# Final feed-forward of a two-layer decode kernel: statistics by small matmuls, column halves in two PSUM banks, a new order of the work

## The chip, the cores and the metric

The kernel runs on one core of one Trainium2 chip. The metric is the device time of one execution in microseconds, as the median of several runs. Engines are named as in the profile: PE is the matrix engine TensorE (PEld its weight loads), DVE is VectorE, ACT is ScalarE, POOL is GpSimd, and SP is SyncE, whose queue issues all the loads here.

## What is computed

Two layers of a decode step for a batch of 8 rows of width 448. Each layer is attention with a cached window, and then a feed-forward with SiLU. Both layers use the same weights and the same cache.

```python
x = A_x                                             # (8, 1, 448), bf16
x = x + _A_ref(_layernorm(x), k_cache, v_cache, wq, wo)
x = x + _B_ref(_layernorm(x), w1, w2)
x = x + _A_ref(_layernorm(x), k_cache, v_cache, wq, wo)
x = x + _B_ref(_layernorm(x), w1, w2)               # the final feed-forward

# _layernorm: (x - mean) / sqrt(var + 1e-5), no scale or shift
# _A_ref: 16 query heads, 8 key/value heads of 256, the last 1024 of 4096 positions;
#         softmax(q k^T / 16) v, then wo (4096 x 448)
# _B_ref: silu(x @ w1) @ w2 with w1 (448 x 1792) and w2 (1792 x 448)
```

Keys and values of the window are 8 rows x 8 heads x 1024 x 256 in bf16, each, which is 64 loads of 512 KB for the keys and 64 for the values. Each is read from HBM once and used by both layers.

## The kernel before

**Rows and layers.** For each batch row b the program builds `layer1(b)` and then `layer2(b)` (L953 to L957). `layer1` transposes the row's key tiles on DVE (L914), computes scores (L641), softmax (`softmax`, L652), the value products (`pv_rows`, L685, and `pv_cols`, L719), and the output projection (`wo_part`, L762). `layer2` begins with `chain` (L793), which holds the first feed-forward of that row and the queries of layer 2, then come scores, softmax and value products of layer 2. All of this is for one row, so matmuls have one or two active columns in the stationary operand and are packed four to the array by `tile_position`. The second output projection and the final feed-forward are done at the end for all eight rows together, in `final_wo` (L835) and `final_rows` (L846).

**The load queue.** Key and value loads go in a fixed sequence into 30 slots of SBUF. A load waits until the tile that was in its slot has been used by both layers. Weights are loaded once, at the beginning.

**What sets the order.** Nothing is ordered by hand. Each step is a `Task` with an engine, a modelled duration, and keys that it reads and writes. PSUM is tracked by whole banks: a step that reads a bank waits for other engines' earlier readers of that bank too (L69 to L75). `Plan.schedule` (L91) is a list scheduler. It gives each task a rank, the length of the modelled path behind it, adds a constant per kind of task (`BIAS`, L25), and lets an engine hold back for a more urgent task that will be ready within `HOLD` times the duration of the one at hand (L24, L141). The resulting order of each engine is emitted as it stands, with semaphore waits between engines. So a change in the tasks, in `OCC` (modelled durations), `BIAS`, `HOLD` or the `rate` of a load can move instructions anywhere in the kernel. Loads keep their sequence.

**Filler matmuls.** `keep` (L773) and `idle` (L779) issue matmuls of zeros that keep TensorE active while it would wait. `keep` writes bank SC[1] and `idle` a bank that it is given.

**The end, step by step.** Eight banks of 512 fp32 columns: SC = 0 and 1 (scores of layers 1 and 2), OB = 2 and 3 (value products), LB = 4 and 5, XB = 6, YB = 7. STB is bank 5.
- `final_wo` sets up the residual in YB (L837) and projects the attention output of all rows, 449 columns in XB, in two parts of 16 matmuls, for the first and the second half of the heads (L839). Column 449 holds the negative mean of the row.
- ACT copies XB to SBUF (L847). Six matmuls fold the four partial sums and turn them into columns (`to_cols`, L537). DVE copies the mean (L852), adds it (L854) and masks (L857), which gives the centred rows `xbt8`.
- `stats8` (L547) computes the variance: squares on ACT (L549), a split in two bf16 parts on DVE (L550, L551), eight matmuls with ones (L556), a scaling (L568), and `pow` on POOL for 128x8 elements (L570), `rhalf8`.
- `up` (L514) multiplies by w1 (16 packed matmuls of 448 columns, L516), ACT copies (L524), five matmuls turn the rows into columns (L527, L529).
- DVE multiplies by `rhalf8` (L861), ACT takes tanh (L864), DVE forms the SiLU (L865).
- 14 packed matmuls multiply by w2 (L867), five bring the residual to XB (L873, L876), ACT copies the product (L878), one matmul adds it to the residual (L879), DVE copies the sum to SBUF (L881), and SP writes it out (L882).

The row sums of w2 and wo, which make the extra column of means, are computed once near the beginning (`row_sums`, L439).

Of the kernel before, what the change touches and what calls it, by code (L numbers as in the profile page):

```python
# [19 lines left out]
       "pe:idle": 0.2296, "act:maskr": 0.13, "act:qbd1": 0.19, "act:var4": 0.16, "act:x2b": 0.16, "act:yrow": 0.50, "act:rsum": 0.66,  # L20
# [3 lines left out]
HOLD, PE_SCALE = 0.563, 1.062  # L24
BIAS = {"dve.KT.a": -19.0, "pe.S0.1.a": 41.7, "pe.oT.a": 213.9, "pe.stat.b": 285.2, "pe.qturn.b": 293.1,  # L25
        "pe.qsel.b": 221.3, "pe.S1.0.b": 186.2, "dve.mb.c": 47.4, "act.exp.c": 84.8, "dve.rl.c": 176.4,
        "pe.PV1.0.1.c": 178.2, "pe.oT.c": 209.3, "pe.idle.e": -29.9}
# [220 lines left out]
def bass_interleave_layers__sliding_block_cached__dense_activation_silu__decode_kernel(  # L248
# [9 lines left out]
    P = 128  # L258
# [64 lines left out]
    z8 = t0f.bitcast(F32)[:, 0:FC * NB]  # L323
    th8 = t1f.bitcast(F32)[:, 0:FC * NB]
    hT8 = t1f[:, 256:256 + FC * NB]
    xbt8 = t1f[:, 400:400 + XC * NB].rearrange("p (c b) -> p c b", b=NB)
# [77 lines left out]
    def load_wq():  # L404
        for c in range(3):
            dma(lambda e, c=c: e.dma_start(wq_sb[:, c * HD:(c + 1) * HD], A_wq[c * P:(c + 1) * P, :]),
                [("wq", c)], P * HD * 2, "wq%d" % c, rate=410e3)
        for h in range(2):
            dma(lambda e, h=h: e.dma_start(wq_sb[64 * h:64 * h + 64, 3 * HD:], A_wq[3 * P:D, h * HD2:(h + 1) * HD2]),
                [("wq", 3 + h)], 32 * HD * 2, "wq%d" % (3 + h), rate=250e3)  # L410

    def load_w1():
        dma(lambda e: e.dma_start(w1_sb[:, 0:3 * F].rearrange("p (c n) -> p c n", c=3),
                                  B_w1[0:3 * P, :].rearrange("(c p) n -> p c n", p=P)),
            [("w1", 0)], 3 * P * F * 2, "w1", rate=390e3)
        for h in range(2):
            dma(lambda e, h=h: e.dma_start(w1_sb[64 * h:64 * h + 64, 3 * F:], B_w1[3 * P:D, h * F2:(h + 1) * F2]),
                [("w1", 1 + h)], 32 * F * 2, "w1%d" % h, rate=250e3)

    def load_wo():  # L420
        dma(lambda e: e.dma_start(wo_sb[:].rearrange("p (c n) -> p c n", n=DP)[:, :, 0:D],
                                  A_wo.rearrange("(c p) n -> p c n", p=P)), ["wo"], HD * D * 2, "wo", rate=380e3)

    def load_w2():
        rows = w2_sb[:].rearrange("p (c n) -> p c n", n=DP)[:, :, 0:D]
        parts = B_w2.rearrange("(j r) n -> j r n", j=4)
        for j in range(4):
            dma(lambda e, j=j: e.dma_start(rows[:, 3 * j:3 * j + 3, :],  # L428
                                           parts[j, 0:3 * P, :].rearrange("(c p) n -> p c n", p=P)),
                [("w2", j)], 3 * P * D * 2, "w2%d" % j, rate=400e3)  # L430
        for h in range(2):
            dma(lambda e, h=h: e.dma_start(rows[64 * h:64 * h + 64, 12:14, :],
                                           parts[h:4:2, 3 * P:D, :].rearrange("j p n -> p j n")),
                [("w2", 4 + h)], P * D * 2, "w2%d" % (4 + h), rate=250e3)
# [4 lines left out]
    def row_sums(w, key, groups, prio):  # L439

        needs = ([("w2", j) for j in range(6)] if key == "w2" else [key]) + H8
# [72 lines left out]
    def up(x, nb, bi, col, reads, prio, fresh):  # L514

        pe([lambda e, c=c, j=j: e.matmul(  # L516
            bank[XB][32 * j:32 * j + nb, 0:D], x(xcol(c, j // 2)), w1_r(j, c), start=(c == 0), stop=(c == KC - 1),
            tile_position=(0, 32 * j), skip_group_check=True) for c in range(KC) for j in range(4)],
           reads + W1_R, bk(XB) + ["part"], (D, 4), prio, "w1")
        if nb == 1:  # L520
            keep(2, prio, "part")
        else:
            idle(2, prio, "part", SC[0])
        act(lambda e: e.activation(qrow[:, 0:D], bank[XB][:, 0:D], ACTF.Copy), bk(XB), ["rowb"], 0.6, prio, "yrow")  # L524
        y = bank[bi][:, col:col + FC * nb].rearrange("p (f b) -> p f b", b=nb)
        pick = ident[:].rearrange("p (j b) -> p j b", b=32)[:, :, 0:nb]
        fns = [lambda e, c=c: e.matmul(y[:, c:12:3, :], qrow[:, c * P:(c + 1) * P], pick, start=fresh, stop=True,  # L527
                                       skip_group_check=True) for c in range(3)]
        fns += [lambda e, h=h: e.matmul(y[64 * h:64 * h + 64, 12:14, :], qrow[:, 3 * P:D], pick[:, h:4:2, :], start=fresh,  # L529
                                        stop=True, tile_position=(0, 64 * h), skip_group_check=True) for h in range(2)]  # L530
        pe(fns, ["rowb", "ident"], bk(bi) + ["turned"], (4 * nb, 1), prio, "yturn")
        if nb == 1:
            keep(2, prio, "turned")
        else:
            idle(4, prio, "turned", SC[0])

    def to_cols(bank_i, col, row, rhs, nb, prio, reads, name, shape):  # L537
        fns = [lambda e, c=c: e.matmul(bank[bank_i][xpart(c), col + c * nb:col + (c + 1) * nb], xpiece(row, c), rhs,  # L538
                                       start=False, stop=True, tile_position=xpos(c), skip_group_check=True)
               for c in range(XC)]  # L540
        fns.append(lambda e: e.matmul(bank[bank_i][:, col + XC * nb:col + (XC + 1) * nb],
                                      row[:, D:D1].broadcast_to([P, P]), rhs, start=False, stop=True,
                                      skip_group_check=True))
        pe(fns, reads, bk(bank_i) + ["folded"], shape, prio, name)


    def stats8(xp, reads, prio, mean):  # L547
# [7 lines left out]
               for c in range(KC)] if mean else []  # L555
# [4 lines left out]
        if mean:  # L560
            dve(lambda e: e.tensor_scalar(nmean8, s1, -1.0 / D, None, op0=ALU.mult), bk(STB), [("qbd", 0, 1)], 0.17, prio)
            dve(lambda e: e.tensor_tensor(vn8, s1, nmean8, ALU.mult), bk(STB) + [("qbd", 0, 1)], [("qbd", 0, 1)], 0.17,
                prio)
            dve(lambda e: e.tensor_tensor(vn8, s2, vn8, ALU.add), bk(STB) + [("qbd", 0, 1)], [("qbd", 0, 1)], 0.17, prio)
            dve(lambda e: e.tensor_scalar(vn8, vn8, D * EPS, 4.0 / D, op0=ALU.add, op1=ALU.mult), [("qbd", 0, 1)],
                [("qbd", 0, 1)], 0.12, prio)
        else:
            dve(lambda e: e.tensor_scalar(vn8, s2, D * EPS, 4.0 / D, op0=ALU.add, op1=ALU.mult), bk(STB),  # L568
                [("qbd", 0, 1)], 0.17, prio)
# [3 lines left out]
    def start_rows(prio):  # L573
# [7 lines left out]
        stats8(xb0[:, 0:XC, :], ["xb0"], prio, True)  # L581
# [103 lines left out]
    def pv_rows(b, layer, k2, prio, oT_dst, oT_key, nj=4):  # L685

        ob, lb, ei = OB[layer], LB[layer], layer
# [105 lines left out]
    def chain(b, prio):  # L793
        xcols(prio)
        stats(YB, C_S2, prio)
        up(lambda c: xbt[:, c:c + 1], 1, YB, C_W1, ["xbt"], prio, False)
# [38 lines left out]
    def final_wo(k2, prio):  # L835
        if k2 == 0:
            pe(lambda e: e.matmul(x8, ident[:], x2b[:].rearrange("p c b -> p (c b)"), start=True, stop=True),  # L837
               ["ident"] + [("x2b", b) for b in range(NB)], bk(YB), (100, 1), prio, "xinit8")
        pe([lambda e, i=i: e.matmul(  # L839
            bank[XB][32 * (i % 4):32 * (i % 4) + NB, 0:D1], oT2[:, i % 2, i // 2, :], wo_sb[:, i * DP:i * DP + D1],  # L840
            start=(i < 4), stop=(i >= NCH - 4), tile_position=(0, 32 * (i % 4)), skip_group_check=True)
            for i in range(16 * k2, 16 * k2 + 16)],
           [(("oT2", b), 2 * h) for b in range(NB) for h in range(4 * k2, 4 * k2 + 4)] + WO_R, bk(XB) + ["part"], (D, 4),
           prio, "wo8")

    def final_rows(prio):  # L846
        act(lambda e: e.activation(rowb, bank[XB][:, 0:D1], ACTF.Copy), bk(XB), ["rowb"], 0.54, prio, "rowb8")  # L847
        idle(2, prio, "part", SC[0])
        to_cols(YB, C_X8, rowb, fold8[:], NB, prio, ["rowb", ] + FOLD8, "fold8", (120, 1))
        idle(2, prio, "folded", SC[0])  # L850
        m58 = mask5[:].unsqueeze(2).broadcast_to([P, XC, NB])
        dve(lambda e: e.tensor_copy(nm8[:], x8[:, XC * NB:]), bk(YB), ["nm8"] + H8, 0.17, prio)  # L852
        xcf = big8[:, 0:XC * NB].rearrange("p (c b) -> p c b", b=NB)
        dve(lambda e: e.tensor_tensor(xcf, x8[:, 0:XC * NB].rearrange("p (c b) -> p c b", b=NB),  # L854
                                      nm8[:].unsqueeze(1).broadcast_to([P, XC, NB]), ALU.add), bk(YB) + ["nm8"], B8, 0.22,
            prio)
        dve(lambda e: e.tensor_tensor(xbt8[:], xcf, m58, ALU.mult), B8 + M5, ["xbt8"], 0.2, prio)  # L857
        stats8(xbt8[:], ["xbt8"], prio, False)
        up(lambda c: xbt8[:, c, :], NB, OB[1], 0, ["xbt8"], prio, True)
        z = z8.rearrange("p (f b) -> p f b", b=NB)  # L860
# [128 lines left out]
```

## Time and profile before

| | us |
|---|---|
| median of 7 runs | 263.03 |
| lowest and highest of them | 261.37, 263.39 |
| the profiled execution's own time | 263.78 |
| its span (first to last instruction) | 262.0 |

| engine | busy us | share of the span | instructions |
|---|---|---|---|
| PE | 197.2 | 75% | 3746 |
| PEld | 101.2 | 39% | 3746 |
| DVE | 153.5 | 59% | 410 |
| ACT | 87.8 | 34% | 241 |
| POOL | 12.8 | 5% | 25 |

The profile is one execution. Its span is shorter than its own time by the 1.78 us before the first and after the last instruction. The loads move 77.67 MB from HBM and are busy in nearly all of the first 222 us; the last 40 us have only compute. PE's busy time includes the filler matmuls (L775 and L782, 33.6 us). A group of instructions is named by its line, its engine and its tiles; "idle before" is the time that the engine stood still ahead of them, with what ended it. The chain is the work that ended last, followed back from the last instruction, at each step to what released it.

### The profile page before, as it was taken

The numbers are of one execution on the slowest core, as the hardware profiler recorded it, in microseconds if no ns is written. First come the engines' busy times: TensorE is split into PE (matmuls) and PEld (weight loads), VectorE is DVE, ScalarE is ACT, GpSimd is POOL, SyncE is SP. The second block draws the span as 40 slices with busy tenths as digits, with TensorE's granted clock in tenths as the row PEclk, the third lists the DMA queues.
The fourth block names the chain that finished last, engine by engine and source line by source line (L and its number), as shares of the span: only waits on it lengthen the run. The fifth ranks groups of instructions, "written<-read, shape, count | busy, mean of one in ns | idle before, by whom it ended". The sixth has DMA issues, their size and how long they took to land.

```text
span 262.0 us, 8450 instructions
## 1 busy us (share of the span) xinstructions
PE 197.2 (75%) x3746; PEld 101.2 (39%) x3746; DVE 153.5 (59%) x410; ACT 87.8 (34%) x241; POOL 12.8 (5%) x25
## 2 busy tenths in 40 slices
PE   0053212399878987999899799979988997998784
PEld 0051100143444454444444454544445444533431
DVE  6468657806964874786388468738863974202221
ACT  2002346624232523441443325244323433132221
POOL 1200000000000000000000000000000000000001
PEclk9999999999999999999999999999999999799999
DMA  6999999999999999998999899999999997000000
GB/s 239 350 403 375 311 339 349 361 362 407 356 354 407 378 317 345 409 361 273 381 402 350 269 405 379 303 319 408 361 293 375 402 350 237 3 3 3 0 3 1
DMA packets 50227, 78.21 MB, mean 299 GB/s; under 512 B 2304, under 2 KB 41104, under 8 KB 49808
## 3 DMA queue, kind: packets, MB, share of 16 engines
q1 hardware_dynamic: 50192, 77.68, 85.1%
q8 instruction: 29, 0.48, 0.8%
q14 instruction: 6, 0.05, 0.0%
HBM read 77.67 MB, written 0.01 MB: 296 GB/s over the span
## 4 chain that ended last, share of the span: by engine, by line
PE 62%; DVE 9%; ACT 9%; SPq 8%; DMA 7%; issue 3%; POOL 1%; DVEq 0%; ACTq 0%
PE bank L699 13%; PE bank L641 13%; DMA wo_sb<-in_A_wo_dram 7%; PE bank L775 6%; PE bank L816 6%; SPq L428 5%; PE bank L768 5%; ACT qbd L662 4%; PE bank L516 3%; DVE qbd L447 3%; PE bank L803 2%; ACT qrow L823 2%; DVE mseg L648 2%; PE bank L709 2%; PE bank L538 2%
## 5 line engine op out<-in xcount | busy, mean ns | idle before, releaser
L914 DVE STREAM_TRANSPOSE slot<-slot 128x512 uint32<-128x512 uint32 x128 | 82.1, 686 | 5.4 <-DMA slot<-in_A_k_cache_dram 5.0
L699 PE MATMUL bank<-slot,pT_sb 128*2 128x256 bf16 x960 | 41.3, 286 | 9.3 <-DMA slot<-in_A_v_cache_dram 8.5
L641 PE MATMUL bank<-slot,qbd 128*8 128x256 bf16 x1024 | 39.7, 284 | 7.0 <-DVE slot L914 6.1
L699 PEld LDWEIGHTS bank<-slot,pT_sb 128*2 128x2 bf16 x960 | 19.7, 84 | 21.5 <-DMA slot<-in_A_v_cache_dram 10.2
L641 PEld LDWEIGHTS bank<-slot,qbd 128*8 128x8 bf16 x1024 | 21.3, 85 | 15.3 <-DVE slot L914 7.2
L662 ACT ACTIVATE qbd<-bank,mseg 128x256 bf16<-128x256 f32 x32 | 12.7, 472 | 37.6 <-DVE mT L654 27.9
L707 ACT ACTIVATE qbd<-bank 128x256 bf16<-128x256 f32 x32 | 12.2, 382 | 30.8 <-PE bank L699 29.3
L648 DVE TENSOR_REDUCE mseg<-bank 128x1 f32<-128x256 f32 x32 | 13.5, 424 | 14.1 <-PE bank L641 13.4
L768 PE MATMUL bank<-wo_sb,oT 128*1 128x449 bf16 x256 | 19.9, 379 | 1.9 <-DVE wo_sb L450 1.9
L775 PE MATMUL bank<-wq_sb,cols_b 128*128 128x512 bf16 x64 | 20.5, 404 | 0.0
L753 POOL TENSOR_TENSOR rhalf<-var,nhalf 128x1 f32<-128x1 f32 x16 | 8.7, 542 | 219.9 <-ACT var L751 219.9
L667 PE MATMUL bank<-ident,qbd 128*128 128x128 bf16 x64 | 6.6, 227 | 16.3 <-ACT qbd L662 16.3
L610 ACT ACTIVATE qbd<-bank,mask 128x128 bf16<-128x128 f32 x32 | 12.2, 381 | 18.3 <-PE bank L605 17.5
L680 DVE TENSOR_REDUCE l_sb<-bank 128x16 f32<-128x64 f32 x16 | 3.6, 225 | 23.4 <-PE bank L675 23.4
L816 PE MATMUL bank<-wq_sb,xbt 128*1 128x512 bf16 x256 | 16.7, 378 | 0.6 <-DVE xbt L742 0.6
L713 DVE TENSOR_TENSOR oT<-bank,l_sb 128x16 bf16<-128x16 f32 (+1 forms) x32 | 6.5, 202 | 16.3 <-PE bank L709 16.0
L782 PE MATMUL bank<-wq_sb,cols_b 128*128 128x512 bf16 x49 | 13.1, 381 | 0.0
L823 ACT ACTIVATE qrow<-bank 128x512 bf16<-128x512 f32 x16 | 9.6, 597 | 9.2 <-PE bank L816 9.2
L667 PEld LDWEIGHTS bank<-ident,qbd 128*128 128x128 bf16 x64 | 3.7, 99 | 22.0 <-ACT qbd L662 22.0
L447 DVE TENSOR_REDUCE qbd<-wo_sb 128x5 f32<-128x2240 bf16 x4 | 9.7, 2479 | 3.7 <-DMA wo_sb<-in_A_wo_dram 3.7
L788 ACT ACTIVATE qrow<-bank 128x449 bf16<-128x449 f32 x8 | 4.4, 548 | 18.1 <-PE bank L768 18.1
L624 DVE TENSOR_TENSOR qbd<-bank,maskr 128x256 bf16<-128x256 f32 x16 | 6.8, 425 | 5.5 <-PE bank L619 5.1
(135 smaller groups left out, 214.8 us busy)
## 6 DMA issues: line engine op xcount, KB each, us to landing
slot<-in_A_k_cache_dram SPq DMA_DIRECT2D x64, 512.0 KB, 10.4
slot<-in_A_v_cache_dram SPq DMA_DIRECT2D x64, 512.0 KB, 8.7
wo_sb<-in_A_wo_dram SPq DMA_DIRECT2D x1, 3584.0 KB, 17.6
wq_sb<-in_A_wq_dram SPq DMA_DIRECT2D x3, 1024.0 KB, 6.9
w_sb<-in_B_w_dram SPq DMA_DIRECT2D x4, 336.0 KB, 15.9
w_sb<-in_B_w_dram SPq DMA_DIRECT2D x1, 1344.0 KB, 11.3
wq_sb<-in_A_wq_dram SPq DMA_DIRECT2D x2, 256.0 KB, 10.2
w_sb<-in_B_w_dram SPq DMA_DIRECT2D x4, 112.0 KB, 8.7
```

The costliest lines, as they stand in the source:

```text
L428: dma(lambda e, j=j: e.dma_start(rows[:, 3 * j:3 * j + 3, :], parts[j, 0:3 * P, :].rearrange("(c p) n -> p c n", p=P)), [("w2", j)], 3 * P ...
L447: dve(lambda e, view=view, n=n, row=row: e.tensor_reduce(row[:, 0:n], view[:, :, 0:D], AX.X, ALU.add, negate=True), needs, [("sums", key, ...
L641: fns.append(lambda e, cb=cb, par=par, j=j, kvh=kvh, kv=kv: e.matmul(bank[sc][32 * j:32 * j + 8, k2 * 256:(k2 + 1) * 256], qbd[qi][:, kvh, ...
L648: dve(lambda e: e.tensor_reduce(mseg[layer][:, k2:k2 + 1], bank[sc][:, k2 * 256:(k2 + 1) * 256], AX.X, ALU.max, negate=True), bk(sc), [("m ...
L662: act(lambda e, k2=k2: e.activation(e_sb[ei][:, k2, :, :].rearrange("p uh (jj ul) -> p uh jj ul", ul=4), bank[sc][:, k2 * 256:(k2 + 1) * 2 ...
L699: fns.append(lambda e, q=q, uh=uh, j=j, vv=vv: e.matmul(bank[ob][32 * j:32 * j + 2, c0:c0 + DH], pT_sb[ei][:, k2 * 2 + uh, j * 8 + 2 * q:j ...
L768: fns.append(lambda e, i=i, c=c, kvh=kvh: e.matmul(bank[XB][32 * c:32 * c + 1, 0:D1], oT1[:, i % 2, i // 2:i // 2 + 1], wo_sb[:, i * DP:i ...
L775: pe([lambda e: e.matmul(bank[SC[1]][:], zero_b.broadcast_to([P, P]), wq_sb[:, 0:512], start=False, stop=True, skip_group_check=True) for ...
L782: pe(lambda e: e.matmul(bank[bi][:], zero_b.broadcast_to([P, P]), wq_sb[:, 0:512], start=False, stop=True, skip_group_check=True), [("wq", ...
L816: pe([lambda e, j=j, c=c, k2=k2, wb=wb: e.matmul(bank[wb][32 * j:32 * j + 1, :], xbt[:, xcol(c, k2):xcol(c, k2) + 1], wq_sb[:, c * HD + (( ...
L823: act(lambda e, wb=wb: e.activation(qrow[:], bank[wb][:], ACTF.Copy), bk(wb), ["rowb"], 0.55, prio, "qrow")
L914: dve(lambda e, v=v: e.transpose(v, v), [("slot", s)], [("slot", s)], 0.67, prio, "KT")
```

## The change

In `final_wo` and `final_rows`:
- The output projection, the product with w1 and the product with w2 are each computed in two column halves, 0 to 255 in one bank and the rest in another (XB or OB[0], and SC[1]). ACT copies the first half and DVE the second (`two`).
- The mean is added by TensorE: one more matmul in `to_cols`, which broadcasts the mean column over all column groups, and one more in the setup of the residual. DVE then only masks.
- The variance comes from 16 small matmuls of the centred rows with themselves (`gram8`); DVE picks the diagonal with an accumulating instruction (`diag8`); POOL takes the power of one column instead of eight.
- The deviation is applied as the scale of the copies of the w1 product (`yrow8`), per row, before the rows are turned into columns. tanh and SiLU then read PSUM.
- The residual and the last sum are in two halves too, in XB and YB, and both engines copy them.

Outside of the final part: the second value half of layer 2 of the last row uses bank OB[0] instead of OB[1]; the row sums also wait for `q1T`; `OCC`, `HOLD`, `BIAS` and the modelled rates of the weight loads have new values.

```diff
@@ planner constants
-HOLD, PE_SCALE = 0.563, 1.062
-BIAS = {"dve.KT.a": -19.0, "pe.S0.1.a": 41.7, "pe.oT.a": 213.9, "pe.stat.b": 285.2, "pe.qturn.b": 293.1,
-        "pe.qsel.b": 221.3, "pe.S1.0.b": 186.2, "dve.mb.c": 47.4, "act.exp.c": 84.8, "dve.rl.c": 176.4,
-        "pe.PV1.0.1.c": 178.2, "pe.oT.c": 209.3, "pe.idle.e": -29.9}
+HOLD, PE_SCALE = 0.837, 1.062
+BIAS = {"dve..e": -51.1, "pe.qsel1.a": -37.9, "pe.S0.0.a": -128.5, "act.exp.a": -58.6, "pe.l.a": 18.8, "act..a":
+        -106.8, "act.oev.a": -58.1, "pe.oT.a": 43.2, "pe.wo.a": -42.9, "pe.stat.b": 263.8, "pe.qturn.b": 188.6,
+        "pe.qsel.b": 262.3, "dve.max.b": 218.8, "dve.mT.c": 118.3, "dve.mg.c": 108.3, "dve.mb.c": 87.2,
+        "act.pTev.c": -93.6, "act.oev.c": -59.6, "pe.oT.c": -79.9, "pe.PV1.1.0.c": -83.7, "pe.PV1.1.2.c":
+        -139.0, "pe.PV1.1.3.c": -36.7, "pe.wo8.c": -95.5, "pe.idle.e": -7.4, "dve.nm8.e": -11.1, "pe.xres.e":
+        -10.8}
@@ load_w1, for one (wq, wo and w2 likewise)
-            [("w1", 0)], 3 * P * F * 2, "w1", rate=390e3)
+            [("w1", 0)], 3 * P * F * 2, "w1", rate=340e3)
@@ row_sums
-        needs = ([("w2", j) for j in range(6)] if key == "w2" else [key]) + H8
+        needs = ([("w2", j) for j in range(6)] if key == "w2" else [key]) + H8 + ["q1T"]
@@ to_cols
+        if nb > 1:
+            fns.append(lambda e: e.matmul(
+                bank[bank_i][:, col:col + XC * nb].rearrange("p (c b) -> p c b", b=nb), row[:, D:D1].broadcast_to([P, P]),
+                rhs.unsqueeze(1).broadcast_to([P, XC, nb]), start=False, stop=True, skip_group_check=True))
@@ pv_rows
-        ob, lb, ei = OB[layer], LB[layer], layer
+        ob, lb, ei = OB[layer] if b < NB - 1 or k2 == 0 else OB[0], LB[layer], layer
@@ final_wo
+        for half, bi, n0, n1 in ((0, XB, 0, 256), (1, SC[1], 256, D1)):
+            pe([lambda e, i=i, bi=bi, n0=n0, n1=n1: e.matmul(
+                bank[bi][32 * (i % 4):32 * (i % 4) + NB, n0:n1], oT2[:, i % 2, i // 2, :],
+                wo_sb[:, i * DP + n0:i * DP + n1], start=(i < 4), stop=(i >= NCH - 4), tile_position=(0, 32 * (i % 4)),
+                skip_group_check=True) for i in range(16 * k2, 16 * k2 + 16)],
...
+    def two(ba, bb, n, dst, keys, prio, name, scale=None):
+
+        sc = 1.0 if scale is None else scale[:, 0:1]
+        rd = [] if scale is None else ["rhalf"]
+        act(lambda e: e.activation(dst[:, 0:256], bank[ba][:, 0:256][0:dst.shape[0]], ACTF.Copy, scale=sc), bk(ba) + rd,
+            [keys[0]], 0.42, prio, name)
+        dve(lambda e: e.tensor_scalar(dst[:, 256:n], bank[bb][:, 256:n][0:dst.shape[0]], sc, None, op0=ALU.mult),
+            bk(bb) + rd, [keys[1]], 0.36, prio, name)
@@ final_rows
-        act(lambda e: e.activation(rowb, bank[XB][:, 0:D1], ACTF.Copy), bk(XB), ["rowb"], 0.54, prio, "rowb8")
+        dve(lambda e: e.memset(g8, 0.0), [], bk(STB), 0.12, prio, "pick8")
+        dve(lambda e: e.memset(pick8, 4.0 / D), [], ["pick8"] + Z8, 0.12, prio, "pick8")
+        for q in range(4):
+            dve(lambda e, q=q: e.tensor_scalar(pick8[32 * q:32 * q + NB, :], fold8[32 * q:32 * q + NB, :], 4.0 / D, None,
+                                               op0=ALU.mult), FOLD8 + ["pick8"], [("pick8", q)], 0.12, prio, "pick8")
+        two(XB, SC[1], D1, qrow, ROW2, prio, "rowb8")
...
-        stats8(xbt8[:], ["xbt8"], prio, False)
-        up(lambda c: xbt8[:, c, :], NB, OB[1], 0, ["xbt8"], prio, True)
+        dve(lambda e: e.tensor_tensor(xbt8[:], x8[:, 0:XC * NB].rearrange("p (c b) -> p c b", b=NB), m58, ALU.mult),
+            bk(YB) + M5, ["xbt8"] + H8, 0.22, prio, "xbt8")
+        dve(lambda e: e.tensor_copy(nm8[:], x8[:, XC * NB:]), bk(YB), ["nm8"], 0.17, prio - 0.1, "nm8")
+        pe([lambda e, c=c, j=j: e.matmul(g8[32 * j:32 * j + NB, :], xbt8[:, c, :], xbt8[:, c, :], start=(c == 0),
+                                         stop=(c == KC - 1), tile_position=(0, 32 * j), skip_group_check=True)
+            for c in range(KC) for j in range(4)], ["xbt8"], bk(STB), (64, 1), prio, "gram8")
+        dve(lambda e: e.scalar_tensor_tensor(out=scr8, in0=g8, scalar=D * EPS, in1=pick8, op0=ALU.add, op1=ALU.mult,
+                                             accum_out=var4[:]), bk(STB) + [("pick8", q) for q in range(4)], ["var4"] + Z8, 0.2, prio, "diag8")
+        add("pool", lambda e: e.tensor_tensor(rhalf[:], var4[:], nhalf[:, 0:1], ALU.pow),
+            reads=["var4", "nhalf"], writes=["rhalf"], dur=0.4, prio=prio, name="pow")
+        for bi, n0, n1 in ((XB, 0, 256), (SC[1], 256, D)):
+            pe([lambda e, c=c, j=j, bi=bi, n0=n0, n1=n1: e.matmul(
+                bank[bi][32 * j:32 * j + NB, n0:n1], xbt8[:, xcol(c, j // 2), :], w1_r(j, c)[:, n0:n1], start=(c == 0),
+                stop=(c == KC - 1), tile_position=(0, 32 * j), skip_group_check=True) for c in range(KC) for j in range(4)],
+               ["xbt8"] + W1_R, bk(bi) + ["part"], (256, 4), prio, "w18")
...
+        two(XB, SC[1], D, qrow, ROW2, prio, "yrow8", rhalf)
+        turn(OB[1], 0, NB, ROW2, prio)
...
-        z = z8.rearrange("p (f b) -> p f b", b=NB)
-        dve(lambda e: e.tensor_tensor(z, bank[OB[1]][:, 0:FC * NB].rearrange("p (f b) -> p f b", b=NB),
-                                      rhalf8.unsqueeze(1).broadcast_to([P, FC, NB]), ALU.mult),
-            bk(OB[1]) + [("qbd", 0, 1)], Z8, 0.25, prio + 0.2)
+        act(lambda e: e.activation(th8, y, ACTF.Tanh), bk(OB[1]), D8, 0.3, prio + 0.2, "th8")
+        dve(lambda e: e.scalar_tensor_tensor(out=hT8, in0=th8, scalar=1.0, in1=y, op0=ALU.add, op1=ALU.mult),
+            bk(OB[1]) + D8, H8, 0.25, prio + 0.2, "hT8")
...
-        dve(lambda e: e.tensor_copy(orow, ops), bk(XB), B8, 0.5, prio + 0.3)
+        two(XB, YB, D, orow, H8, prio + 0.3, "out9")
```

## The prediction

> **What bounds the kernel now.** I read the page, then the chain of work that ended last, then the waits of the load queue, then the DMA rate over one batch row, then the clock in short stretches.
>
> The page gives the chain's shares:
>
> ```profile
> PE 62%; DVE 9%; ACT 9%; SPq 8%; DMA 7%; issue 3%; POOL 1%; DVEq 0%; ACTq 0%
> ```
>
> TensorE carries the chain, but with small matmuls and with hops to ScalarE and VectorE. Is it compute or the loads that set the pace of a row? The waits of the load queue and the DMA rate in 176 to 202 us (40 slices of 0.65 us, busy tenths and GB/s) answer:
>
> ```profile
> SPq L472 <- PE bank L641: 32.0, 7, 5.8
> ```
>
> ```profile
> DMA  9999999999999999999999999983499899989999
> GB/s 403 422 391 416 410 397 416 384 422 403 416 411 397 380 359 356 353 350 350 343 350 348 350 348 348 336 285 131 139 367 347 232 315 377 364 347 391 441 384 397
> ```
>
> The reader is to see the dip near 193.5 us. Once per row the loads run dry for over a microsecond, because the next V load waits until the layer-2 scores (L641) have released a K slot. So a row of about 23.9 us (the softmax exponentials start at 148.14, 172.01, 195.94 and 219.90) is a loop of compute, slot release and load, without slack. Work moved within this loop counts seven times, once for each period between rows.
>
> The last loads land near 222 us; after that only compute is left. Its end, in the chain in order of time (start, us, what):
>
> ```profile
> 247.62 0.39 ACT qbd L707
> ...
> 248.34 0.97 PE bank L699 x32
> ...
> 250.53 0.96 PE bank L839 x16
> 251.52 0.56 ACT qrow L847
> ...
> 252.63 0.18 DVE qbd L852
> 252.83 0.21 DVE qbd L854
> 253.07 0.21 DVE qbd L857
> ...
> 253.32 0.93 PE bank L516 x16
> 254.25 0.30 PE bank L556 x8
> 254.58 0.18 DVE qbd L568
> ...
> 254.82 1.66 POOL qbd L570
> ...
> 256.57 0.29 DVE qbd L861
> 256.88 0.30 ACT qbd L864
> ...
> 257.29 0.29 DVE qbd L865
> ...
> 257.62 0.94 PE bank L867 x14
> 258.58 0.55 ACT qrow L878
> ...
> 259.18 0.37 PE bank L879
> 259.57 0.61 DVE qbd L881
> ```
>
> One instruction at a time, no engine shared: what is cut here comes off the end in full. The power on GpSimd (L570, 1.66) is the longest piece; the first product has been turned into columns by 255.27, and its scaling (L861) waits for the power until 256.57.
>
> The clock, by stretches (us of the stretch; busy PE, PEld, DVE, ACT, POOL; granted clock; DMA share; GB/s):
>
> ```profile
> 223.00:223.50 0.50, 0.50 (x20) 0.35 (x12) 0.17 (x1) 0.00 (x0) 0.00 (x0) 0.50 0.00 0
> ```
>
> Half clock, from about 222.95 to 226.4. The last row goes from its first value products (221.85) to its first keep-warm pair (229.55) in 7.70 us; row 6 took 6.36 for the same (197.88 to 204.24). So this profile holds 1.34 us of slow clock.
>
> **What the Trainium skill says.** "PSUM — Partial Sum Buffer", on bank collisions: two engines may not touch one bank and 32-partition quadrant at once. So ScalarE and VectorE can share an evacuation only if the halves lie in two banks, as the change puts them; before, one engine reads 449 columns alone (L847, 0.55), and no trace here shows the shared case. "TensorEngine Tiling (Array Packing)", Key Properties: changing the tiling mode drains the array; the trace has idle gaps of 0.2 to 0.4 us put down to issue wherever packed and full-size matmuls alternate (before L709, L729, L775), so I add none between the new Gram matmuls and the packed w1, which share a mode. "TensorE: Matmul & The Clock Gate", Part 1: the clock is halved after a 3.4 us activity window that was too idle, and the windows run free of the kernel; the stretch above, 3.4 us long, agrees.
>
> **The change part by part.** First the unit prices. Sixteen packed matmuls of 256 columns took 0.61, thirty-two took 1.05: 27 ns each beyond the first group. Sixteen of 448 took 0.93. VectorE from PSUM: 0.42 for 256 columns (L648), 0.61 for 448 (L881), 0.17 for 16, so 0.16 + 1.0 ns a column, 0.36 for 192. ScalarE: 0.38 for 256 columns (L707), 0.55 for 449. A scale read from memory costs 0.09 more (L788: 0.55 without, 0.64 with; the skill's page "ScalarE: Activation LUTs", What ACT_TABLE_LOAD costs, says about 93 ns a pointer). The eight-column power took 1.64, the one-column power 0.54 (L753).
>
> *a) Last product of the output projection, its evacuation and centring (250.53 to 253.27, 2.74 us).* The product goes from 0.93 to about 1.05 (32 matmuls for 16). The ScalarE half starts at 0.61 and is covered by the second half; VectorE follows with 0.36 + 0.04 hop, ending at 1.45 against 1.54 now: -0.09. The row fold gets one matmul more, about +0.06 (six there are issued in about 0.35). Of three VectorE steps (L852, L854, L857, 252.63 to 253.27, 0.64) one is left, 40 columns from PSUM, 0.20: -0.44. The copy of the mean goes behind it, under the Gram matmuls. Together -0.47. The two filler matmuls behind the fold end their streaming about when the new operand is ready; if not, +0.1.
>
> *b) From the centred rows to the activated hidden rows (253.27 to 257.57, 4.30 us).* Gone: square, two VectorE steps, eight ones-matmuls, the 1.64 power, the scaling L861. New: 16 Gram matmuls (hop 0.05, then 0.60 as for sixteen small packed ones); the diagonal with its accumulator on VectorE. No row shows that operation. Below it is bounded by 0.17 (any eight-column VectorE row); above by 0.45 (the skill's "VectorE: DVE Perf Modes", Two Vector instructions with no wait between them, makes it two instructions; ScalarE's accumulator read took 0.19). I take 0.25, with 0.04 to start it. Then 0.07 + 0.54 for the one-column power and 0.05 hop: the deviation stands at 1.60. Meanwhile the two w1 halves follow the Gram matmuls and end near 1.53, so both are due together. Evacuation with the scale 0.47, hop 0.06, turn 0.37 (254.90 to 255.27), hop 0.04, tanh 0.30, hop 0.11, product 0.28: 3.23. Saving 1.07.
>
> *c) Second product to the output (257.62 to 260.18).* 28 matmuls for 14: +0.03. Evacuation 0.36 for 0.54: -0.18. Fold of 192 columns for 448: 0.25 for 0.35, -0.10. Last copy in two halves, 0.38 for 0.61: -0.23. Together -0.48. The closing DMA is unchanged.
>
> *d) Layer 2's second value half of the last row gets its own bank.* Now it waits for ScalarE to read the first half: PV ends 247.58, evacuation to 248.00, then the transpose, next PV at 248.27. With another bank it could start about 247.5. But the softmax sum and the transposes must still pass TensorE, each with a drain of about 0.2, and the output projection has 32 matmuls more. Between 0 and -0.7; I take -0.3.
>
> *e) Setup of the diagonal mask and the zeroed bank.* Six small VectorE writes of 0.1 to 0.2, under the output projection or in earlier idle time; 0.1 each if they meet a waiting step. The row sums' new wait on q1T costs nothing: it is written by 20.2 us (L598), the sums start at 30.6.
>
> *f) The new order.* HOLD, biases and rates change, so every queue may be permuted, DVE's, ACT's and PE's; the load queue keeps its sequence but sees its slots released at other times. The profile can't price that. Bounds: one period more or less by 0.4 us is +/-2.8. I take 0. The cover for a shift would be the DMA queue's backlog; the dip says it is used up once a row.
>
> Sum: -0.47 - 1.07 - 0.48 - 0.30 = -2.3. Against the profiled execution's 263.78 (span 262.0 plus 1.78 around it) that is 261.5; that run lies 0.75 above the median of 263.03, so a median of 260.7.
>
> **Rivals.**
> - *The new order shortens the loop.* For it: in the last period the exponentials of row 7 layer 1 wait until 219.90 although its scores ended near 216.3, and TensorE has fillers in its place. Against: the old order had the same chance. At 0.2 to 0.4 us a row, 1.4 to 2.8 more: about 258.6.
> - *Slower: the new order delays the layer-2 scores.* Place: the release of the K slots behind the dip at 193.5. The new biases rank several layer-1 and layer-2 steps by about 100 either way, which can push the scores back. Every 0.1 us adds 0.7. From 0.33 us a row the 2.3 are eaten; at 0.6 it is 263.03 - 2.3 + 4.2 = 264.9. Against: TensorE is 91% busy there, fillers included, so a good order is not hard to keep.
> - *The variance is not early.* If the Gram matmuls are queued behind both w1 halves, as L556 now stands behind L516, the deviation is 0.9 later and b) saves about 0.2: 261.6. Against: the planner ranks by remaining path, and the Gram path is longer.
> - *The clock.* A half-clock window more or less moves +/-1.3, to 262.0 or 259.4. A denser tail speaks for less.
>
> **How the numbers follow.** Plan as worked out, order neutral within 0.15 us a row: 0.50, 260.7, own range 259.6 to 261.8. Shorter loop: 0.21. Variance late or one more slow window: 0.09, 261.6 to 262.2. Order a little worse, gain just eaten: 0.08. Slower loop: 0.12. Within 0.3% (262.24 to 263.82, what a measurement of this kernel can tell from no change): 0.09; faster 0.79; slower 0.12. Range 258.0 to 263.2: it leaves out the slower loop and the far end of the shorter one.
>
> **What would show it.** Right: no 1.6 us power at the end; from the last output projection to the output copy's end 7.6 us instead of 9.65; the Gram matmuls ahead of w1 on PE; ScalarE and VectorE rows of about 0.4 side by side three times; starts of the exponentials still 23.9 apart. Wrong: a period other than 23.9, a half-clock stretch at another place, or the scaled evacuation idle behind the power for over 0.3 us.

## The result, and the profile after

The kernel after takes 258.77 us (median of 12 runs, 257.18 to 261.60), beside 263.02 us for the kernel before (31 runs): a ratio of 0.9846, 95% interval 0.982 to 0.9872, or 4.25 us less. One of the twelve (261.60) counts as a slow run, and the ratio compares fast runs alone. The profiled execution took 257.18 us with a span of 255.0, so it is the fastest of the twelve, while the profiled execution of before lay 0.76 us above its median. Their spans differ by 7.0 us; 1.34 of it is the half-clock stretch in the profile of before. Differences of the two profiles are therefore read stage by stage, not as a whole.

The profile of after has a half-clock stretch too, at another place, as its page shows (40 slices of 6.4 us, the granted clock in tenths):

```profile
PEclk9999995569999999999999999999999999999999
```

It lasts from about 38 to 55 us, where the weights and the first rows are still being loaded. It cost nothing that can be seen: the first exponentials of layer 2 start at 72.59 in after and 71.99 in e10, which both have it, and at 72.49, 72.83 and 73.33 in e6, e7 and e8, which do not.

The chain of the page for the kernel after, to be set against the one shown of before:

```profile
PE 50%; SPq 20%; DMA 11%; DVE 8%; ACT 7%; issue 2%; POOL 0%; ACTq 0%; DVEq 0%
```

TensorE has gone from 62% to 50% of it, and the load queue with its transfers from 15% to 31%. In these two profiles the chain leans more on the loads than before. How much it does varies from profile to profile: with the old order e2 has 57% and 27%, and with the new order e11 has 59% and 19%. The same shows in the waits of VectorE for key tiles between 60 and 215 us (in total, times, longest), first in before, then in after:

```profile
DVE slot L914 <- DMA slot<-in_A_k_cache_dram: 1.0, 2, 0.6
```

```profile
DVE slot L947 <- DMA slot<-in_A_k_cache_dram: 5.6, 11, 1.5
```

These waits vary in the same way: 0.2 to 3.1 us in the five profiles with the old order, 0.3 to 5.6 in the nine with the new one.

The end, in the chain of after (start, us, what):

```profile
240.22 0.85 ACT qbd L664 x2
...
245.00 1.26 PE bank L844 x48
...
247.75 0.24 PE bank L876 x15
...
248.01 0.18 DVE qbd L879 x2
...
248.27 0.56 POOL rhalf L881
...
248.91 0.48 ACT qrow L855
...
249.49 0.23 PE bank L534 x3
```

The 1.66 us power is a 0.56 us one, and the steps between it and the centred rows are two. The Gram matmuls (L876, the centred rows times themselves) stand ahead of the product with w1, as the planner's ranks suggested.

The last stage is better seen in the timeline of after (start, us, engine, line, operation, tiles, count, idle before):

```profile
250.26 0.27 DVE L894 SCALAR_TENSOR_TENSOR qbd<-qbd,bank 128x112 bf16<-128x112 f32 x1 [0.92 <-ACT qbd L893]
...
250.31 0.28 PE L903 MATMUL bank<-ident,qbd 128*8 128x128 bf16 x2
...
250.63 0.39 PE L784 MATMUL bank<-wq_sb,cols_b 128*128 128x512 bf16 x1
...
250.95 0.93 PE L897 MATMUL bank<-w_sb,qbd 128*8 128x256 bf16 x28
...
251.92 0.36 DVE L857 TENSOR_SCALAR qrow<-bank 128x192 bf16<-128x192 f32 x1 [1.40 <-PE bank L897]
...
252.55 0.25 PE L911 MATMUL bank<-qrow,fold 128*8 128x192 bf16 x1
```

The hidden rows are ready at 250.53, but the product with w2 (L897) starts at 250.95: the first half of the residual (L903) and a filler (L784) are queued ahead of it. The residual's second sum (L911) starts 0.27 us after its operand (252.28), behind another filler. In before the product had started 0.05 us after the hidden rows.

Stage by stage, with times from the two timelines (us):

| stage of the end | before | after | difference | forecast |
|---|---|---|---|---|
| last exponentials to the evacuated output projection (a's evacuation, and d) | 7.20 | 6.45 | -0.75 | -0.39 |
| to the centred rows (rest of a) | 1.20 | 0.88 | -0.32 | -0.38 |
| to the hidden rows (b) | 4.30 | 2.98 | -1.32 | -1.07 |
| to the end of the output copy (c) | 2.61 | 2.66 | +0.05 | -0.48 |
| sum | 15.31 | 12.97 | -2.34 | -2.32 |

The last stage gained about what was forecast for its evacuation, fold and last copy (0.18, 0.10 and 0.26 us) and lost it again in two waits on TensorE's queue: 0.37 us more ahead of the product and 0.21 ahead of the second sum.

The time from the last exponentials to the output DMA (15.34 before, 13.06 after) is a good yardstick for the final part: nothing is loaded then, and in three profiles of after it was 13.06 each time.

### The profile page after: what moved, and what is told of

Read it like the earlier page. It is cut to its first block, busy times and chain, and to the rows that moved or that the text cites. A ratio compares the mean times of both kernels' runs of the same rounds, so it can differ in the third digit from the quotient of the medians.

```text
span 255.0 us, 8596 instructions
## 1 busy us (share of the span) xinstructions
PE 190.9 (75%) x3820; PEld 102.0 (40%) x3820; DVE 153.3 (60%) x416; ACT 88.2 (35%) x241; POOL 11.8 (5%) x25
## 4 chain that ended last, share of the span: by engine, by line
PE 50%; SPq 20%; DMA 11%; DVE 8%; ACT 7%; issue 2%; POOL 0%; ACTq 0%; DVEq 0%
PE bank L643 11%; DMA slot<-in_A_k_cache_dram 11%; PE bank L701 9%; SPq L483 6%; PE bank L818 5%; SPq L433 5%; PE bank L770 4%; PE bank L777 4%; ACT qbd L664 3%; SPq L471 3%; DVE mseg L650 3%; SPq L477 2%; PE bank L805 2%; PE bank L521 2%; DVE slot L947 2%
## 5 line engine op out<-in xcount | busy, mean ns | idle before, releaser
L701 PE MATMUL bank<-slot,pT_sb 128*2 128x256 bf16 x960 | 38.2, 279 | 9.4 <-DMA slot<-in_A_v_cache_dram 9.0
L643 PE MATMUL bank<-slot,qbd 128*8 128x256 bf16 x1024 | 39.0, 281 | 4.9 <-DVE mseg L650 2.5
L701 PEld LDWEIGHTS bank<-slot,pT_sb 128*2 128x2 bf16 x960 | 20.4, 83 | 18.5 <-DMA slot<-in_A_v_cache_dram 8.9
L643 PEld LDWEIGHTS bank<-slot,qbd 128*8 128x8 bf16 x1024 | 20.8, 85 | 13.2 <-DVE mseg L650 4.3
L777 PE MATMUL bank<-wq_sb,cols_b 128*128 128x512 bf16 x64 | 19.4, 384 | 0.0
L650 DVE TENSOR_REDUCE mseg<-bank 128x1 f32<-128x256 f32 x32 | 12.9, 415 | 8.2 <-PE bank L643 7.5
L784 PE MATMUL bank<-wq_sb,cols_b 128*128 128x512 bf16 x49 | 13.5, 382 | 0.0
```

Source lines behind the costliest of these rows:

```text
L643: fns.append(lambda e, cb=cb, par=par, j=j, kvh=kvh, kv=kv: e.matmul(bank[sc][32 * j:32 * j + 8, k2 * 256:(k2 + 1) * 256], qbd[qi][:, kvh, ...
L650: dve(lambda e: e.tensor_reduce(mseg[layer][:, k2:k2 + 1], bank[sc][:, k2 * 256:(k2 + 1) * 256], AX.X, ALU.max, negate=True), bk(sc), [("m ...
L701: fns.append(lambda e, q=q, uh=uh, j=j, vv=vv: e.matmul(bank[ob][32 * j:32 * j + 2, c0:c0 + DH], pT_sb[ei][:, k2 * 2 + uh, j * 8 + 2 * q:j ...
L777: pe([lambda e: e.matmul(bank[SC[1]][:], zero_b.broadcast_to([P, P]), wq_sb[:, 0:512], start=False, stop=True, skip_group_check=True) for ...
L784: pe(lambda e: e.matmul(bank[bi][:], zero_b.broadcast_to([P, P]), wq_sb[:, 0:512], start=False, stop=True, skip_group_check=True), [("wq", ...
```

## The experiments

Theory A: the final part gives about 2.3 us, and the new order gives the rest by shortening the rows. Rivals: the order is neutral and the final part gives it all, or order and final part only pay together. The order of the rows' loop in e1 is that of after, and in e2 that of before; they differ only around the last row's value products and output projection, and in the setup of the diagonal mask on VectorE. Here "old order" and "new order" stand for these two.

**e1, the new order alone**

```diff
-HOLD, PE_SCALE = 0.563, 1.062
+HOLD, PE_SCALE = 0.837, 1.062
...
-        needs = ([("w2", j) for j in range(6)] if key == "w2" else [key]) + H8
+        needs = ([("w2", j) for j in range(6)] if key == "w2" else [key]) + H8 + ["q1T"]
```

(with BIAS and load rates of after.)

> The kernel before with the new order alone: its HOLD, biases and load rates, and the wait of the row sums on q1T; the old final part stays. Theory A, that final part and order add up: about 2.0 us less than the kernel before (the 4.25 us of the whole change less the 2.3 of the final part), with a row period near 23.5 us in the profile instead of 23.9. Rival B, that the order is neutral and the profiles differ by chance: within 0.5 us of the kernel before. Rival C, that the new order only pays together with the new final part: slower than before.

262.08 us beside 262.69: ratio 0.9976, interval 0.9953 to 1.0. That is only 0.6 us where theory A expected 2.0, and the row period is not near 23.5 (table below). The time alone does not decide between the three. The profile shows one reason: from the last exponentials to the output DMA it takes 15.88 us, 0.54 more than before. With the old final part the new order puts half of the output projection into the middle of the last value products.

**e2 and e9, the new final part with the old order**

```diff
-HOLD, PE_SCALE = 0.837, 1.062
+HOLD, PE_SCALE = 0.563, 1.062
```

(with BIAS and load rates of before.)

> The kernel after with the old HOLD, biases and load rates: its order in the rows' loop is that of the kernel before, the final part is new. Theory A: 2.0 to 2.6 us less than before, with the exponentials still 23.9 us apart and 12.9 us from the last exponentials to the end of the output copy instead of 15.3. Rival B: the whole 4.25 us less. Rival C: under 1 us less.

> The kernel of e2 once more, beside after, to size the order's share where both carry the new final part. Theory A2, the order makes a row without loads 0.4 us shorter but the rows with loads then wait for their keys: 1 to 2 us more than after, and 23.6 us in the profile from the exponentials of the last loaded row to those of the last row, against 23.2. Rival B: equal to after within 0.5 us, and the whole gain is the final part.

260.36 us beside 262.69 (ratio 0.9885, 0.9845 to 0.9924), and again 260.51 beside 262.68 (0.991, 0.9883 to 0.9937): 2.2 to 2.3 us less than before, 13.11 us in both profiles from the last exponentials to the output DMA. The final part with the old order is worth what the sum of the prediction said, and no more.

**e5 and e10, after once more**

> The kernel after, unchanged, beside the next three and for a second profile. Theory A (final part and order add up): 4.0 to 4.4 us less than before; 13.1 us from the last exponentials to the output DMA as in its first profile, and a period of 23.3 to 23.7 us. If its first profile was a lucky one: the period is nearer 23.9.

> The kernel after once more, as the partner of e9 and of the next two. Theory A2: 1 to 2 us less than e9; 13.06 us from the last exponentials to the output DMA, as twice before, and VectorE waiting several times for key loads within the rows. Rival B: equal to e9 within 0.5 us.

258.49 us (ratio 0.9863, 0.9815 to 0.9912) and 258.61 us (0.9845, 0.9791 to 0.99). Measured side by side, e10 is 1.9 us below e9, so with the new final part the order is worth 1.9 us. All runs of after together (258.59) against all of e2 and e9 (260.51) give the same. The rival of a neutral order falls. e5 was as expected in its time and in its final part, but its period is 23.84, near the 23.9 named for the case that the first profile was a lucky one.

Where the 1.9 comes from is read from the exponentials of the softmax. One point needs care. Early in the new order a row's four exponentials stand in two pairs, so the mark is their end, and not the start of one or the other pair. First e9, then after:

```profile
73.84 0.84 ACT L661 ACTIVATE qbd<-bank,mseg 128x256 bf16<-128x256 f32 x2 [4.75 <-DVE mseg L657]
...
100.62 1.57 ACT L661 ACTIVATE qbd<-bank,mseg 128x256 bf16<-128x256 f32 x4 [4.94 <-DVE mT L653]
```

```profile
72.59 0.84 ACT L664 ACTIVATE qbd<-bank,mseg 128x256 bf16<-128x256 f32 x2 [5.10 <-DVE mseg L660]
...
98.50 0.84 ACT L664 ACTIVATE qbd<-bank,mseg 128x256 bf16<-128x256 f32 x2 [4.65 <-DVE mseg L660]
99.50 0.84 ACT L664 ACTIVATE qbd<-bank,mseg 128x256 bf16<-128x256 f32 x2 [0.16 <-DVE mseg L660]
```

In the table (us), "first stretch" goes from the end of the first layer-2 exponentials (about 74 us) to the end of those at about 100. The period is the mean over the five that follow, from end to end, and the last row goes from start to start.

| kernel | first stretch | period of a loaded row | last row | last exponentials to output DMA | median |
|---|---|---|---|---|---|
| before | 27.54 | 23.91 | 24.97 (half clock) | 15.34 | 263.02 |
| e2, final part only | 27.77 | 23.85 | 23.65 | 13.11 | 260.36 |
| e9, the same | 27.51 | 23.83 | 23.52 | 13.11 | 260.51 |
| after | 26.91 | 23.66 | 23.16 | 13.06 | 258.77 |
| e5, the same | 26.85 | 23.84 | 23.19 | 13.06 | 258.49 |
| e10, the same | 26.89 | 23.76 | 23.20 | 13.06 | 258.61 |
| e1, order only | 26.89 | 24.08 (one row at half clock) | 23.24 | 15.88 | 262.08 |

- The first stretch is 0.7 us shorter. This repeats best: 27.51 to 27.77 in the five profiles with the old order, 26.80 to 26.91 in the nine with the new one.
- The five periods are 0.09 shorter on average, 0.4 in all, and in e5 they are no shorter than in e9. Four of the five periods of after are 23.63 or 23.64; the shortest of e9 is 23.80.
- The last row is 0.4 shorter.

Together this is 1.5 of the 1.9. The rest would lie ahead of 74 us, where e2 and e9, the same kernel, already differ by 2.1 us, so it can't be placed. What in the order shortens the first stretch was not tested alone. In after, TensorE takes the scores of row 1 (L643, 74.04) ahead of the value products of row 0; in e9, 16 value products (L698, 75.50) stand ahead of the same scores (L640, 75.94).

The last row has no loads, so there the order shows bare. TensorE's timeline in e9 and then in after, row 7 (softmax sums L674 and L677, transposes of the value products L708 and L711 are full-size; the rest is packed four to the array):

```profile
221.71 0.61 PE L698 MATMUL bank<-slot,pT_sb 128*2 128x256 bf16 x16
222.25 0.23 PE L674 MATMUL bank<-pT_sb,cols_b 128*128 128x64 bf16 x2
222.42 1.04 PE L698 MATMUL bank<-slot,pT_sb 128*2 128x256 bf16 x32
223.39 0.23 PE L674 MATMUL bank<-pT_sb,cols_b 128*128 128x64 bf16 x2
223.56 0.61 PE L698 MATMUL bank<-slot,pT_sb 128*2 128x256 bf16 x16
224.10 0.21 PE L708 MATMUL bank<-ident,qbd 128*128 128x8 bf16 x2
...
224.99 0.21 PE L708 MATMUL bank<-ident,qbd 128*128 128x8 bf16 x2
...
226.00 0.21 PE L708 MATMUL bank<-ident,qbd 128*128 128x8 bf16 x2
...
227.96 0.60 PE L774 MATMUL bank<-wq_sb,cols_b 128*128 128x512 bf16 x2
```

```profile
219.01 0.61 PE L701 MATMUL bank<-slot,pT_sb 128*2 128x256 bf16 x16
219.55 0.29 PE L677 MATMUL bank<-pT_sb,cols_b 128*128 128x64 bf16 x4
219.77 1.48 PE L701 MATMUL bank<-slot,pT_sb 128*2 128x256 bf16 x48
...
221.31 0.21 PE L711 MATMUL bank<-ident,qbd 128*128 128x8 bf16 x2
...
222.80 0.38 PE L711 MATMUL bank<-ident,qbd 128*128 128x8 bf16 x4
...
224.94 0.60 PE L777 MATMUL bank<-wq_sb,cols_b 128*128 128x512 bf16 x2
```

Five separate full-size groups have become three. From the exponentials to the pair of fillers (L774, L777) it is 8.20 us in e9 (219.76 to 227.96) and 7.88 in after (217.06 to 224.94). How much of the 0.32 is due to the merged groups is asked next.

**e3 and e4, single moves of the order**

e3 and e4 are e2 with the planner's lists edited for rows 2 to 7:

```diff
@@ e3: VectorE transposes the row's last key tile ahead of the first maximum
...
+        pl.order["dve"] = o[:n] + [kt, o[n], mx] + o[n + 1:]
@@ e4: the softmax sum of layer 1 goes ahead of its value products
+        move("pe", ["%da.l" % b], "%da.PV0.%d.0.0" % (b, b))
+        move("dve", ["%da.lsum" % b, "%da.rl" % b], "%dc.lsum" % (b - 1))
```

> As e2, but in rows 2 to 7 VectorE transposes the last key tile before it takes the maximum of the first half of the scores, as in the new order. If this move is what shortens the period (the transposes no longer stand behind a maximum that waits for TensorE): 1.5 to 2 us less than e2, period 23.5. If the period is set by something else: within 0.4 us of e2.

> As e2, but in rows 2 to 7 the softmax sum of layer 1 goes ahead of its value products on TensorE, and its reciprocal first on VectorE, as in the new order: the two sums then stand together and one change of tiling mode goes. If this move shortens the period: 0.2 to 0.4 us a row, 1.2 to 2.4 us less than e2. If not: within 0.4 us of e2.

e3 took 260.90 us (ratio 0.9911, 0.9879 to 0.9944), so this move does not shorten the rows; two of its periods are 23.80 and 23.81, as in e9. e4 took 260.10 us (0.9887, 0.9852 to 0.9921), within the 0.4 us of e2 that was expected if the move does not shorten the period. Its profile still shows a small effect. The two sums stand together, and the pair of fillers starts 8.12 us after the exponentials, against 8.20 in e9:

```profile
222.24 0.29 PE L674 MATMUL bank<-pT_sb,cols_b 128*128 128x64 bf16 x4
...
227.86 0.60 PE L774 MATMUL bank<-wq_sb,cols_b 128*128 128x512 bf16 x2
```

It is 8.12 in five of the six rows. So one full-size group less is worth 0.08 us of the 0.32. The other 0.24 came with the paired transposes and the regrouped output projection, which were not run by themselves.

The profile of e3 has a half-clock stretch of its own, in another row than that of before (stretch in us, busy PE, PEld, DVE, ACT, POOL, granted clock, DMA share, GB/s):

```profile
199.00:202.00 3.00, 3.00 (x52) 1.50 (x50) 0.95 (x4) 0.39 (x1) 0.00 (x0) 0.52 1.04 408
```

That row took 25.36 us (196.39 to 221.75), about 1.5 more than its neighbour.

**e7, the Gram matmuls late**

```diff
+    n = max(i for i, t in enumerate(o) if t.name == "w18")
+    o.insert(n + 1, g)
```

> The kernel after with the Gram matmuls behind both halves of the product with w1 on TensorE, instead of ahead. If the power's path sets the scaled evacuation: it starts 0.6 to 0.8 us later and the kernel takes that much longer than after. If the product's own path sets it: no change, or 0.3 us less.

259.47 us (ratio 0.9893, 0.9845 to 0.9941), 1.0 more than e5 beside it, and 13.85 us from the last exponentials to the output DMA, 0.79 more. The chain of e7:

```profile
249.54 0.87 PE bank L884 x31
250.88 0.56 POOL rhalf L881
251.52 0.48 ACT qrow L855
```

The power starts behind the product, and the scaled evacuation (the copy from PSUM, L855) follows it at once. It starts 9.51 us after the last exponentials instead of 8.69. So here the power's path sets the start, and Gram matmuls that stand ahead are worth 0.8 us.

**e8, the last value products in one bank**

```diff
-        ob, lb, ei = OB[layer] if b < NB - 1 or k2 == 0 else OB[0], LB[layer], layer
+        ob, lb, ei = OB[layer], LB[layer], layer
```

> The kernel after with the second value half of the last row back in the bank of the first half. If the bank is worth what the two profiles suggest (0.75 us up to the evacuation, 0.09 of it from the column halves): 0.4 to 0.7 us more than after. If the softmax sum, the transposes and the drains between tiling modes fill the place: under 0.2 us.

260.32 us (ratio 0.9915, 0.9888 to 0.9942), and 14.18 us to the output DMA, 1.12 more than after: more than either theory said. The chain of e8, and then two lines of the timeline of after:

```profile
244.17 1.07 PE bank L701 x32
245.25 0.02 issue
245.27 0.39 ACT qbd L709
245.66 0.13 issue
245.79 0.19 PE bank L711 x2
245.98 0.54 PE bank L701 x16
246.52 0.77 PE bank L844 x32
247.29 0.46 PE bank L701 x16
```

```profile
241.88 1.05 PE L701 MATMUL bank<-slot,pT_sb 128*2 128x256 bf16 x32 [0.37 <-ACT pT_sb L673]
...
243.01 0.61 PE L701 MATMUL bank<-slot,pT_sb 128*2 128x256 bf16 x16
```

The second half starts 1.81 us after the first, against 1.13 in after (241.88 to 243.01): 0.68 of waiting for ScalarE's read. And the planner, which knows of that wait, puts 32 matmuls of the output projection (0.77 us) in the middle of the value products. The remaining 0.44 goes with that; it was not separated. The medians of e8 and e5 differ by 1.8 us, 0.7 more than this stretch accounts for, and where that lies is open.

**e6, e11 and e12, the order of the last stage**

```diff
@@ e6: the product with w2 ahead of the residual and the third filler
+    ... o[:turn + 1] + idles[:2] + w28 + late + idles[2:3] + rest[:1] + idles[3:4] + rest[1:] + idles[4:]
@@ e11: the two sums ahead of the fillers too
+    ... o[:turn + 1] + idles[:2] + named["w28"] + named["xres"] + named["fold9"] + idles[2:]
@@ e12: and one filler instead of two ahead of fold8 and of gram8
```

> The kernel after with one change of order on TensorE in the final part: the two halves of the product with w2 stand directly behind the turn and its two fillers, ahead of the residual's matmuls and a third filler. In the profile of after the product starts 0.42 us behind the hidden rows that it needs, of which about 0.37 is these matmuls. If that is why the third stage gained nothing: 0.3 to 0.4 us less than after, and the product starts within 0.1 us. If the stage is held by something else, or the residual is then late: within 0.1 us of after.

> As e6, but the two matmuls that add the second product to the residual follow the residual directly and the fillers stand behind them. In e6 the second of them began 0.76 us after its operand was there, behind fillers. If the fillers ate the gain of e6: 12.4 to 12.6 us from the last exponentials to the output DMA instead of 13.06, and about 0.6 us less than after. If the residual's matmuls themselves are late: 12.8 or more.

> As e11, with one filler instead of two ahead of the row fold and one instead of two ahead of the Gram matmuls. In the profile of after these fillers end 0.1 us after their followers could start. If they delay: about 0.15 us less than e11, 12.3 us from the last exponentials to the output DMA. If the followers' own waits set it: equal to e11. If the clock is halved in the final part for want of activity: over 1 us more.

e6 took 259.06 us, no less than after, with 13.18 us to the output DMA. Its timeline says why:

```profile
253.08 0.36 DVE L857 TENSOR_SCALAR qrow<-bank 128x192 bf16<-128x192 f32 x1 [1.03 <-PE bank L897]
...
254.20 0.25 PE L911 MATMUL bank<-qrow,fold 128*8 128x192 bf16 x1
```

The product started in time, and then the second sum came 0.76 us after its operand (253.44), behind fillers. In e11 its weights are loaded 0.04 us after its operand (252.70):

```profile
252.34 0.36 DVE L857 TENSOR_SCALAR qrow<-bank 128x192 bf16<-128x192 f32 x1 [1.03 <-PE bank L897]
...
252.51 0.48 PE L911 MATMUL bank<-qrow,fold 128*8 128x256 bf16 x2
```

(the second of these two matmuls loads its weights at 252.74). e11 has 12.48 us to the output DMA, 0.58 less than after, as expected; in the median it took 258.35 (ratio 0.9841, 0.979 to 0.9892) beside 258.61, too little to tell by time alone. e12 has 12.40 and took 257.52 us (ratio 0.9812, 0.9759 to 0.9864), 1.1 less than after beside it; the intervals of the two overlap. Its expectation was 0.15 less than e11; the profile shows 0.08, so the rest of the 0.8 between the two medians is not explained by the final part. No half clock fell into the final part of its profile. e12 is the fastest version here, by median and by final part.

## Why the prediction was right, and where not

The direction and the range held; the value did not. The final part came as worked out, and the new order added 1.9 us that the prediction had put at nothing. 258.77 lies 1.9 us below the predicted 260.7, outside the likeliest case's own range.

- *a) to d), the final part: right as a sum.* 2.32 forecast, 2.34 in the profiles, 2.2 to 2.3 in e2 and e9. Their 260.4 and 260.5 us are near the predicted 260.7. The terms were less good than their sum:
  - b) gained 1.32 for 1.07. The mis-sized term is the 16 Gram matmuls, put at 0.60 by the nearest row with 256 columns; they took 0.26. The diagonal, put at 0.25 between 0.17 and 0.45, took 0.17 with its accumulator read.
  - c) gained nothing for 0.48. "28 matmuls for 14: +0.03" counted the product's own length, not what is queued ahead of it: the residual and fillers on TensorE, which nothing had waited for before. e11 gives it back.
  - d) was put at 0.30 from 0 to 0.7. In the first stage of the end 0.75 appears for d) and the evacuation together, and e8 loses 1.12 without the bank; beyond the wait this holds a planner's answer to it.
- *f), the new order: wrong.* "I take 0" should have been -1.9. For the loaded rows themselves, "order neutral within 0.15 us a row" was right (0.09 on average, by the end of the exponentials). What the term left out is everything else that the same order moves: the stretch ahead of 100 us (0.7) and the last row (0.4).
- *The shorter loop*, which gave "about 258.6", hit the number by luck. It put 0.2 to 0.4 us into each of seven periods; five loaded periods gave 0.09 each. Its place was wrong too. The exponentials of row 7 still follow both layers' scores; what shrank is the stretch behind them. The prediction read the drains off the trace but did not ask whether the new order would change their number.
- *No cover:* the loop was said to be without slack, so that each cut counts in every row. That does not hold. The stretch behind the exponentials is 0.32 us shorter in all six rows of after, the last row is 0.4 shorter, and the periods of the loaded rows only 0.09. That the loads take up part of what compute gives would fit VectorE's longer waits for keys in after, but these waits vary from profile to profile, so it is not shown.
- *The slower rival* did not come: the V loads' waits for released key slots went from 32.0 to 27.8 us (29.7 to 34.4 in five profiles with the old order, 26.6 to 32.3 in nine with the new). *The late variance* did not come, and e7 shows that it would have cost 0.8, near the 0.9 named.
- *A half-clock stretch at another place* was named as a sign of being wrong. It came, at 38 to 55 us, and cost nothing that can be seen.

Why the order brought only 0.6 us in e1 and 1.9 with the new final part is explained in part. The profile of e1 has the shorter first stretch and the shorter last row too. The gains of the order seen above, 1.5 us, less the 0.54 that its final part lost leave about 1.0. That lies within e1's interval (0 to 1.2 us). So order and final part add up except at the end, where the old final part and the new order do not fit.

## What to carry to other kernels

When a chain at the end is rebuilt, list what the in-order queue holds ahead of each critical instruction, fillers too: a stage shortened by 0.5 us gained nothing until its residual and fillers were moved behind. A list scheduler's order can be worth nearly as much as the rebuilt step itself, and its gain need not lie in the steady rows: compare the beginning and the last row too. Mark a period by the same event in every profile, and ask whether a group that serves as the mark has been split. Check a sum term by term and by a yardstick that repeats (here a stretch without loads, 13.06 us three times) where the whole time scatters by 2 us.

## What the runs showed of the hardware

- Sixteen packed matmuls with 8 columns on both sides took 0.26 us in all, where sixteen of 256 columns take 0.61; their weight loads took 0.15.
- A VectorE operation with an accumulator shows as two entries, 0.17 and 0.08 us, which overlap: the pair ends 0.17 us after its start. A scale read from memory made a 192-column VectorE copy 0.42 us long instead of 0.36.
- One full-size group less between packed matmuls was worth 0.08 us a row (e4, 8.12 against 8.20).
- Stretches of half clock of about 3.4 us fell into one row in some profiles (before at 223, e3 at 199) and made that row 1.3 to 1.5 us longer. A stretch of 17 us, in after at 38 to 55 us, cost nothing visible: TensorE was busy for 5.8 of these 17 us, and for 6.0 of them in e6 at full clock.
- Half clock is not the only cause of the scatter of 2 us between runs. Six runs of after had a clock of 1.0 throughout and still took 257.68 to 261.60 us. In e2 and e9, the same kernel at a clock of 1.0 and 0.999, the difference is there before 74 us (72.59 and 74.69), while the weights and the first rows are loaded; its cause was not found.
